# An adaLN block with a spectral filter and a gated feed-forward: the filtered product's planes added on GpSimd, mirrored W columns in rising order, powers on GpSimd, new orders

## The chip, the cores and the metric

The kernel runs on one core of one Trainium2 chip. The metric is the device time of one execution in microseconds. Engines are called PE (TensorE), PEld (its weight load), DVE (VectorE), ACT (ScalarE), POOL (GpSimd) and SP (SyncE, here the DMA queue).

## The reference, cut to what matters

```python
mod = (silu(c) @ w_mod).reshape(1, 6, 1, -1)      # sa, ca, ga, sb, cb, gb
h = layernorm(x) * (1 + ca) + sa                  # x: 1 x 2048 x 640
x = x + ga * irfft2(rfft2(h) * (w_r + 1j * w_i))  # filter over both axes
h = layernorm(x) * (1 + cb) + sb
x = x + gb * ((silu(h @ w_gate) * (h @ w_up)) @ w_down)   # 640 -> 1728 -> 640
```

All tensors are bfloat16; the transforms are done as matrix products with tables of cosines and sines.

## The kernel before, in words

The 2048 rows are 16 tiles of 128. Four stages follow each other, and each of the first three is driven by an order written out by hand: a string of short names, each of which issues the instructions of one step. An engine runs its own instructions in that order, so the string sets what stands behind what on every engine and on SP's DMA queue.

Stage 1 (to about 34 us) normalises the tiles and does the transform along the 640 axis and the first part of that along the rows; ACT writes the result into `A_sb`. GpSimd scales the table rows there (`gscale`, L305 and L306); tile 14's scaling runs on DVE.

Stage 2, the filter stage (34 to about 70 us), runs over 17 units (unit 16 is a small rest). For a unit `u`:
- `B`/`T`,`t`: turn a piece of `A_sb`, by a DMA transpose of two units (`B`, L424) or on PE with a copy (`T`, L431, and `t`, L437).
- `X`, `Xe`: eight matmuls with the tables (L451 to L459), copied from PSUM by ACT (L466).
- `P`: the product with the filter W on DVE, two instructions (L484): 768 elements a partition with columns of `Wb`, 512 with mirrored columns of `Wq`, which are read in falling order. The result `PP` has two planes that have to be summed.
- `Y`, `y`: five blocks turned by PE with the identity, two matmuls for each block, one for each plane, which sum in PSUM as float32 (L498, L502); the copy `y` goes to ACT for odd units and to DVE for even ones (L509).
- `E`, `e`: six matmuls with the inverse tables (L525 to L533) and a strided copy into `Ep` (L543), on ACT but for unit 14 and half of 15.

`J` and `Je` build `Wq` from `Wb` (matmuls L586, copies L589), `W` and `Jn` negate parts of the filter, `m` mirrors `Ep` (all L259 on DVE). `Ri` (L580) folds the gate ga into `Rinv_sb`; ga is turned and goes through DRAM to be spread over the partitions (L241, L247). `sb` and `cb` at the end compute two more modulation vectors on PE (L226). PSUM tiles come from a ring of four slots, so a step that needs a slot waits until the fourth one before it has been copied out.

Stage 3, the way back: `s` (ten matmuls, L659), `V` (ACT copy, L666), `d` (five matmuls, L672), `x` (DVE: add the input, with row sums, L675), `n` (mean, L679), `q` (ACT: squares, L683). `rt` takes the root for tiles 0 to 3 (ACT, then DVE's reciprocal and bias, L686 to L688), `xn`/`xa` normalise, `T`/`f` turn and scale them (L724, L728, L730). `gA` and `g0` to `g7` begin the feed-forward part of the first four tiles; `N` and a later call take the inverse roots of the other tiles on DVE by Newton steps (`ln2_newton`); `mb`, `mt` and `w` fold the gate gb into the down weights.

Stage 4 is the feed-forward part for the rest: `ffn_mm` (L764), `ffn_silu` (L769), `ffn_mul` (L773) and the down product (L852, L865), four passes of four tiles.

Of the kernel before, what the change touches and what calls it, by code (L numbers as in the profile page):

```python
# [22 lines left out]
NC5 = 5  # L23
# [82 lines left out]
def adaln_block_kernel(  # L106
# [29 lines left out]
    modcols = const.tile([P, 2, NC5], F32, name="modcols")  # L136
# [4 lines left out]
    neg1 = const.tile([P, 1], F32, name="neg1")  # L141
    ssq, vm = (const.tile([P, NT, 2], F32, name=n) for n in ("ssq", "vm"))
# [39 lines left out]
    nc.vector.memset(Wq[:, 3 * NT * 128:], 0.0)  # L182
    nc.vector.memset(Wqp[:, 1, 0:2048:64], 0.0)
# [36 lines left out]
    nc.gpsimd.memset(PP64[:], 0.0)  # L220
    nc.scalar.activation(warm[:], eps_t[:], ACT.Silu)
# [192 lines left out]
    with tc.tile_pool(name="ph2", bufs=2, reuse_waits="tile") as ph2, \  # L414
         tc.tile_pool(name="ps2", bufs=4, space=bass.MemoryType.PSUM, reuse_waits="tile") as ps2:
        B2all = big.tile([P, 8, NR, 128], BF16, name="B2all", tag="gt")
        B64 = ph2.tile([P, 2, 128], BF16, name="B64", bufs=1)
        X64 = ph2.tile([P, NI], BF16, name="X64", bufs=1)
# [14 lines left out]
        def copy_t(u):  # L433
            n = 640 if u < 16 else 256
            ps = pss.pop(("t", u))
            o = (B2all[:, u % 8] if u < 16 else B64[:]).rearrange("p b q -> p (b q)")
            (nc.vector.tensor_copy if u in (0, 1) else nc.scalar.copy)(o, ps[:, 0:n])  # L437
# [22 lines left out]
        def copy_x(u):  # L460
            xps = pss.pop(("x", u))
            if u == 16:
                nc.scalar.copy(X64[:], xps[:, 0, 0:NI])
                return
            X = Xs[u] = ph2.tile([P, NI, 4], BF16, name="X", bufs=6)
            nc.scalar.copy(X[:].rearrange("p q (b j) -> p q b j", b=2),  # L466
                           xps[:, :, 0:2 * NI].rearrange("p b (j q) -> p q b j", j=2))

        def product(u):
# [35 lines left out]
        def copy_y(u):  # L505
            yf = pss.pop(("y", u))[:].rearrange("p b q -> p (b q)")
# [28 lines left out]
        def copy_e(u):  # L535
# [5 lines left out]
            def put(s0, j0, n, copy=nc.vector.tensor_copy if u == 14 else nc.scalar.copy):  # L541
# [24 lines left out]
        def mods_cb(_):  # L566
            m = mods(wm_g, 1)
            nc.scalar.copy(modcols[:, 1, :], m)
            nc.scalar.add(one_p_cb[:], m, 1.0)

        def mods_sb(_):
            nc.scalar.copy(modcols[:, 0, :], mods(wm_sb, 0))
# [9 lines left out]
        def turn_w(h):  # L582
            ps = pss["j", h] = slot("wps")
            wv = Wb[:, 1 - h // 2, :, 0:256].rearrange("p k (m l) -> p k m l", m=2)
            for b in range(2):
                nc.tensor.matmul(ps[:, b, :], lhsT=jrev[:], rhs=wv[:, 8 * (h % 2) + 4 * b:8 * (h % 2) + 4 * b + 4, :, 64:128], start=True, stop=True)  # L586
# [5 lines left out]
        def loads(i):  # L592
# [49 lines left out]
    ps3 = ctx.enter_context(tc.tile_pool(name="ps3", bufs=4, space=bass.MemoryType.PSUM, reuse_waits="tile"))  # L642
    xsum, mean2, sq2, rstd2 = (const.tile([P, NT], F32, name=n) for n in ("xsum", "mean2", "sq2", "rstd2"))
# [3 lines left out]
    def ring(name):  # L647
        return ps3.tile([P, 2, 512], F32, name=name, tag="f")
# [29 lines left out]
    def ln2_mean(t):  # L678
        nc.vector.tensor_scalar(mean2[:, t:t + 1], xsum[:, t:t + 1], 1.0 / D, None, ALU.mult)  # L679

    def ln2_square(t):
        junk = ph4.tile([P, D], BF16, name="junk2", bufs=1)
        nc.scalar.activation(junk[:], x1[:, t, :], ACT.Square, scale=-1.0, bias=mean2[:, t:t + 1], accum_out=sq2[:, t:t + 1])  # L683

    def ln2_root(_):
        nc.scalar.activation(rstd2[:, 0:4], sq2[:, 0:4], ACT.Sqrt, bias=eps_t[:], scale=1.0 / D)  # L686
# [4 lines left out]
    def silu_table(_):
        nc.scalar.activation(warm[:], rstd2[:, 3:4], ACT.Silu)

    def ln2_newton(a, b):
        I32 = mybir.dt.int32
        n = b - a
        v = ph4.tile([P, 8], F32, name="veps")[:, 0:n]
        nc.vector.tensor_scalar(v, sq2[:, a:b], 1.0 / D, EPS, ALU.mult, ALU.add)
        yi = ph4.tile([P, 8], I32, name="rs_yi")[:, 0:n]
        nc.vector.tensor_single_scalar(yi, v.bitcast(I32), 1, ALU.arith_shift_right)  # L700
        nc.vector.tensor_scalar(yi, yi, -1, 0x5F3759DF, ALU.mult, ALU.add)
        y = yi.bitcast(F32)
        tt = ph4.tile([P, 8], F32, name="rs_t")[:, 0:n]
        for it in range(3):
            nc.vector.tensor_tensor(tt, y, y, ALU.mult)
            nc.vector.scalar_tensor_tensor(tt, tt, -0.5, v, ALU.mult, ALU.mult)
            nc.vector.scalar_tensor_tensor(rstd2[:, a:b] if it == 2 else y, tt, 1.5, y, ALU.add, ALU.mult)

    def ln2_xn(t):
# [3 lines left out]
        nc.vector.tensor_scalar(xn2s[sc][:, tl, :], x1[:, t, :], mean2[:, t:t + 1], rstd2[:, t:t + 1], ALU.subtract, ALU.mult)  # L713
# [66 lines left out]
    def gb_mods(_):  # L780
        mg_ps = ring("mg_ps")
        mod_cols(mg_ps[:, 0], wm_gb)
        nc.scalar.copy(g_col[1][:], mg_ps[:, 0, 0:MW * NC5:MW])
# [8 lines left out]
    def at_of(sc):  # L792
        if len(AT2) <= sc % 2:
# [6 lines left out]
             "m": lambda f: ffn_mul(AT2[0], f), "mA": lambda _: ffn_mul13(0, AT2[0]), "wm": silu_table, "N": lambda _: ln2_newton(4, 8), "mb": gb_mods, "mt": gb_turn, "w": fold}  # L800
    plan = (
# [152 lines left out]
```

## Time and profile before

| | us |
|---|---|
| median of 3 runs (lowest, highest) | 271.76 (271.46, 274.04) |
| the profiled execution | 272.35 |
| its span | 270.5 |
| PE, DVE, ACT, POOL busy | 260.0, 150.5, 122.2, 21.4 |
| granted clock | 1.00 |

The span is what the profile covers; the execution is 1.85 us longer. Times in the views count from the start of the span. A matmul's row shows its latency, while the next one starts before it has ended; what a step costs PE is therefore read from start to start. A group's row gives busy time, mean of one, then the idle time of the engine before it and what ended that.

### The profile page before, as it was taken

What the parts mean: (1) busy time and instruction counts of PE and PEld (TensorE: products, weight loads), DVE (VectorE), ACT (ScalarE), POOL (GpSimd) and SP (SyncE); (2) the same over time, 40 slices, a digit from 0 to 9 for tenths busy, and PEclk for the clock granted to TensorE, in tenths of its full rate; (3) what the DMA queues carried; (4) which work ended last, traced back from release to release, by engine and by line L of the source; (5) the groups of instructions that cost most, each with busy time, mean ns of one, the idle gap of its engine ahead of it and who ended that gap; (6) DMA issues with size and microseconds to landing.
All of it is one profiled execution on the core that took longest, in us unless ns stands there. A gap on an engine that the chain in (4) does not pass through costs nothing.

```text
span 270.5 us, 5340 instructions
## 1 busy us (share of the span) xinstructions
PE 260.0 (96%) x2190; PEld 168.3 (62%) x2190; DVE 150.5 (56%) x359; ACT 122.2 (45%) x221; POOL 21.4 (8%) x44
## 2 busy tenths in 40 slices
PE   6899999999978999999999999999999999999994
PEld 6788869988966555456644446654445664444663
DVE  2599979989388569984425452524344342333151
ACT  5499679898699976422033223022223103322000
POOL 3378800000000000000000000000000000000000
PEclk9999999999999999999999999999999999999999
DMA  7999457899397001040210004110004011000011
GB/s 245 334 344 357 138 142 175 220 233 335 104 396 283 10 14 24 0 97 2 74 34 13 0 0 97 51 58 10 2 0 97 2 73 34 12 0 0 0 51 48
DMA packets 35422, 27.80 MB, mean 103 GB/s; under 512 B 18117, under 2 KB 32710, under 8 KB 35270
## 3 DMA queue, kind: packets, MB, share of 16 engines
q1 hardware_dynamic: 35396, 27.46, 33.0%
q8 instruction: 17, 0.28, 0.4%
q14 instruction: 7, 0.06, 0.1%
q10 hardware_dynamic: 2, 0.00, 0.0%
HBM read 20.37 MB, written 2.62 MB: 85 GB/s over the span
## 4 chain that ended last, share of the span: by engine, by line
PE 75%; DMA 13%; DVE 4%; ACT 4%; SPq 2%; issue 1%; DVEq 0%; ACTq 0%
PE gu L764 42%; PE oa L865 20%; DMA Wb<-in_A_w_i_dram 5%; DMA x_sb<-in_A_x_dram 4%; PE va L659 2%; DMA wm_g<-in_w_mod_dram 2%; PE gu L751 2%; DMA ga_row<-gTa 1%; DVE late L675 1%; DMA ga_bc<-ga_row 1%; PE m_ps L226 1%; PE yps L498 1%; PE oa L852 1%; PE oab L672 1%; SPq L207 1%
## 5 line engine op out<-in xcount | busy, mean ns | idle before, releaser
L773 DVE TENSOR_TENSOR AT<-gu,sg 128x512 bf16<-128x512 f32 x52 | 35.8, 689 | 54.2 <-ACT sg L769 54.2
L764 PE MATMUL gu<-h2T_all,Wg 128*128 128x512 bf16 x260 | 64.6, 379 | 0.0
L764 PE MATMUL gu<-h2T_all,Wu 128*128 128x512 bf16 x260 | 64.6, 379 | 0.0
L769 ACT ACTIVATE sg<-gu 128x512 f32<-128x512 f32 x52 | 31.0, 596 | 70.0 <-PE gu L764 68.4
L865 PE MATMUL oa<-late,AT 128*128 128x320 bf16 x403 | 56.1, 299 | 0.0
L865 PEld LDWEIGHTS <-AT 128*128 128x128 bf16 x429 | 40.8, 98 | 17.2 <-issue 1.4
L764 PEld LDWEIGHTS <-Wu 128*128 128x128 bf16 x260 | 25.4, 98 | 30.7
L764 PEld LDWEIGHTS <-Wg 128*128 128x128 bf16 x260 | 25.1, 98 | 29.3
L879 DVE TENSOR_TENSOR xo<-oa,late 128x320 bf16<-128x320 f32 x31 | 20.0, 695 | 31.8 <-PE oa L852 18.6
L675 DVE SCALAR_TENSOR_TENSOR late<-oab,x_sb 128x640 bf16<-128x640 f32 x16 | 14.1, 884 | 10.2 <-PE oab L672 10.1
L753 ACT ACTIVATE sg<-gu 64x512 f32<-64x512 f32 x4 | 2.3, 586 | 37.2 <-PE gu L751 37.2
L305 POOL TENSOR_SCALAR Gs<-Gtab,rstd 128x256 bf16<-128x256 bf16 x15 | 13.8, 923 | 11.6 <-DVE rstd L300 8.2
L317 DVE SCALAR_TENSOR_TENSOR Z<-rtile,vm,z 128x640 bf16<-128x640 f32 x16 | 13.9, 872 | 0.4 <-PE z L312 0.3
L683 ACT ACTIVATE junk<-late,mean 128x640 bf16<-128x640 bf16 x16 | 13.2, 828 | 0.3
L330 ACT CAST A_sb<-aps 128x650 bf16<-128x650 f32 x16 | 11.1, 706 | 2.5 <-PE aps L326 2.3
L281 ACT COPY early<-t1ps 128x640 bf16<-128x640 bf16 x13 | 9.0, 692 | 5.9 <-PE t1ps L278 5.5
L466 ACT CAST X<-xps 128x640 bf16<-128x640 f32 x16 | 10.8, 696 | 1.6 <-PE xps L459 1.0
L659 PE MATMUL va<-Htab,Ep 128*128 128x128 bf16 x160 | 10.7, 219 | 0.8 <-ACT VT L666 0.4
L666 ACT CAST VT<-va 128x640 bf16<-128x640 f32 x16 | 10.5, 696 | 1.3 <-PE va L659 1.3
L659 PEld LDWEIGHTS <-Ep 128*128 128x128 bf16 x160 | 9.8, 118 | 1.0 <-issue 0.8
L498 PE MATMUL yps<-identb,PP 128*128 128x128 bf16 x130 | 9.7, 219 | 0.2 <-DVE Y L509 0.2
L325 PE MATMUL aps<-Z,Gs 128*128 128x325 bf16 x32 | 9.2, 303 | 0.0
(292 smaller groups left out, 337.6 us busy)
## 6 DMA issues: line engine op xcount, KB each, us to landing
x_sb<-in_A_x_dram SPq DMA_DIRECT2D x8, 320.0 KB, 6.2
out_dram<-xo SPq DMA_DIRECT2D x15, 160.0 KB, 1.7
Wu<-in_B_w_up_dram SPq DMA_DIRECT2D x1, 2080.0 KB
late<-in_B_w_down_dram SPq DMA_DIRECT2D x1, 2080.0 KB
wm_g<-in_w_mod_dram SPq DMA_DIRECT2D x2, 800.0 KB, 5.6
Wb<-in_A_w_r_dram SPq DMA_DIRECT2D x1, 1284.0 KB, 10.3
Wb<-in_A_w_i_dram SPq DMA_DIRECT2D x1, 1284.0 KB
Wg<-in_B_w_gate_dram SPq DMA_DIRECT2D x1, 1280.0 KB
```

The source lines that it names most:

```text
L305: e.tensor_scalar(Gss[t][:, 0:2], Gtab[:, t], rstd1[:, t:t + 1], None, ALU.mult)
L317: nc.vector.scalar_tensor_tensor(Zs[t][:].rearrange("p r q -> p (r q)"), rv, vm[:, t, 1:2], held.pop(("z", t))[:, 0:D], ALU.mult, ALU.add)
L330: (nc.vector.tensor_copy if t in A_DVE else nc.scalar.copy)(A_sb[:, :, t, :, :], i)
L498: nc.tensor.matmul(yf[:, 128 * j:128 * j + 128], lhsT=PP[:, cp, 0:128] if u == 16 else PP[:, cp, 0:128, j], rhs=identb[:], start=(cp == 0) ...
L659: nc.tensor.matmul(vf[:, 128 * r:128 * r + 128], lhsT=Ep[:, t, 65 - 65 * g:193 - 65 * g, r], rhs=Htab[:, t, g, :], start=(f == 1 and r in ...
L675: nc.vector.scalar_tensor_tensor(x1[:, t, :].rearrange("p (r a) -> p r a", r=NR), VTs.pop(t).rearrange("p (r a) -> p r a", r=NR), 1.0, x_s ...
L683: nc.scalar.activation(junk[:], x1[:, t, :], ACT.Square, scale=-1.0, bias=mean2[:, t:t + 1], accum_out=sq2[:, t:t + 1])
L764: nc.tensor.matmul(o, lhsT=w_[:, c5, fc * 128:(fc + 1) * 128], rhs=h2T_all[:, sc % 2, :, c5, :], start=(c5 == 0), stop=(c5 == NC5 - 1))
L769: nc.scalar.activation(gus[fc][1][:], gus[fc][0][:, 0, :], ACT.Silu)
L773: nc.vector.tensor_tensor(AT[:, fc, :], gu[:, 1, :], sg[:], ALU.mult)
L865: nc.tensor.matmul(o, lhsT=AT[:, fc, tl * 128:(tl + 1) * 128], rhs=Wd_sb[:, fc, h * 320 + d0:h * 320 + d0 + n], start=(fc == 0 and not ear ...
L879: nc.vector.tensor_tensor(xos[tl][:, h * 320:(h + 1) * 320].rearrange("p (a r) -> p a r", r=NR), ps[0][0].rearrange("p (a r) -> p a r", r= ...
```

## The change

- After the product, the two planes of `PP` are added: on GpSimd for eleven units (`Q_POOL`), on DVE for two (`Q_DVE`). For these thirteen, `Y` is five transposes of bf16 data into PSUM as bf16, instead of ten matmuls. `PP` has five buffers instead of four.
- `Wq` is built with the columns already reversed (the matmul `J` reads them with step -1), so that both products read rising columns.
- The copies are dealt out anew: `y` (`Y_ACT`), `t`, `e` (`E_DVE`) and `Je`. Units 2 and 3 are turned by a DMA transpose.
- The Silu table is loaded in stage 2 (`wm`); `sb` and `cb` stand at the head of stage 3's order; the loads of `wm_gb`, Wg and Wd are issued behind them, `wm_gb` first. The PSUM ring is kept over both stages. The write of the ga row goes out on ACT's queue, its spreading is a step of its own (`gs`).
- The inverse root for the second normalisation is an add and a power on GpSimd (`ln2_power`), with the 1/640 put into the squares; root, reciprocal and Newton steps go.
- Both orders are new.

The diff, cut:

```diff
-            for n, off, rows, wd, l, step in ((48, 0, Wbr, 128, l0, 1), (32, 48, Wqr, 64, 0, -1)):
+            for n, off, rows, wd in ((48, 0, Wbr, 128), (32, 48, Wqr, 64)):
...
+        def add(u):
+            PP = PPs[u]
+            (nc.gpsimd if u in Q_POOL else nc.vector).tensor_tensor(PP[:, 0], PP[:, 0], PP[:, 1], ALU.add)
+
         def stage_y(u):
             yps = pss["y", u] = slot("yps")
+            PP = PPs.pop(u)
+            if u in Q_POOL + Q_DVE:
+                yb = yps[:, 0, 0:320].bitcast(BF16)
+                for j in range(4):
+                    nc.tensor.transpose(yb[:, 128 * j:128 * j + 128], PP[:, 0, 0:128, j], identb[:])
+                nc.tensor.transpose(yb[:, 512:640], PP[:, 0, 128:NI].rearrange("p q j -> p (q j)"), identb[:])
+                return
...
         def turn_w(h):
             ps = pss["j", h] = slot("wps")
-            wv = Wb[:, 1 - h // 2, :, 0:256].rearrange("p k (m l) -> p k m l", m=2)
+            w = Wb[:, 1 - h // 2, 8 * (h % 2), 128]
             for b in range(2):
-                nc.tensor.matmul(ps[:, b, :], lhsT=jrev[:], rhs=wv[:, 8 * (h % 2) + 4 * b:8 * (h % 2) + 4 * b + 4, :, 64:128], start=True, stop=True)
+                nc.tensor.matmul(ps[:, b, :], lhsT=jrev[:], 
+                                 rhs=bass.AP(w.tensor, w.offset + 1536 * b, [w.ap[0], [384, 4], [128, 2], [-1, 64]]),
+                                 start=True, stop=True)
...
-        Y_ACT = (1, 3, 5, 7, 9, 11, 13, 15)
-        J_DVE = (0, 1)
+        Y_ACT = (0, 1, 3, 4, 8, 12, 13)
+        T_DVE, E_DVE = (1,), (3, 6, 14)
+        Q_POOL, Q_DVE = (3, 4, 5, 6, 7, 8, 9, 10, 11, 12, 14), (2, 15)
+        J_DVE = (0, 2)
...
+            "J2 T0 T1 t0 J3 Je3 Je2 t1 J0 W0 B2 B4 J1 X0 Je1 Je0 X1 Xe0 Jn W1 Xe1 P0 P1 ga X2 Xe2 gt X3 X4 X5 P2 Xe3 P3 B6 Y0 "
+            "Xe4 Xe5 Y1 Q2 y0 P4 Q3 y1 P5 X6 Xe6 E0 Y2 y2 Y3 Q4 e0 B8 B10 y3 X7 E1 X8 Xe7 W2 P6 e1 X9 Q5 Y4 Xe8 Xe9 Y5 W3 E2 "
+            "y4 e2 X10 P7 E3 P8 Xe10 Q6 y5 P9 e3 X11 T16 E4 Xe11 B12 P10 B14 Q7 Y6 t16 e4 y6 E5 P11 Y7 Q8 X12 Y8 e5 y7 E6 "
+            "Xe12 Q9 X13 y8 m0 e6 Q10 X16 X14 P12 Q11 L2 Y9 Xe13 Q12 y9 P13 Xe16 E7 L1 Xe14 e7 E8 e8 Y10 E9 X15 P16 Y11 y10 "
+            "P14 e9 Y12 Y13 y11 gs Xe15 P15 y12 E10 Y16 Ri E11 y13 Q14 E12 e10 Y14 Q15 e11 y16 L3 e12 Y15 E13 m1 wm y14 e13 "
+            "L4 E16 E14 y15 m2 e16 e14 m3 E15 e15 m4 "
...
+    def ln2_power(a, b):
+        nc.gpsimd.tensor_scalar(sq2[:, a:b], sq2[:, a:b], EPS, None, ALU.add)
+        nc.gpsimd.tensor_tensor(rstd2[:, a:b], sq2[:, a:b], mhalf[:, 0:b - a], ALU.pow)
...
+        "sb sx cb cx s0 s1 s2 V0 d0 s3 V1 s4 x0 V2 V3 n0 d1 d2 V4 q0 s5 x1 s6 n1 x2 V5 d3 n2 x3 V6 q1 d4 s7 d5 V7 s8 x4 "
+        "n3 q2 x5 d6 x6 V8 d7 q3 s9 d8 x7 s10 s11 V9 rt x8 nb V10 V11 s12 xn0 s13 n4 d9 xn1 x9 T0 V12 xn2 s14 V13 n5 xa3 "
+        "f0 T1 s15 V14 f1 d10 V15 mb mx gA d11 x10 x11 n6 n7 q4 g0 z0 mt g1 q5 z1 n8 g2 z2 m0 q6 m1 w0 d12 x12 mA n9 n10 "
+        "m2 q7 g3 g4 d13 n11 z3 m3 x13 q8 q9 w1 z4 m4 n12 g5 n13 w2 q10 N d14 q11 x14 z5 g6 m5 w3 q12 n14 d15 q13 x15 g7 "
+        "z6 n15 q14 q15 z7 m6 m7 "
```

More of the change, by code (lines that the diff above doesn't have):

```diff
@@ L412, in adaln_block_kernel @@
     NPE = 2
[L414 to L415 removed]
+    ps2 = ctx.enter_context(tc.tile_pool(name="ps2", bufs=4, space=bass.MemoryType.PSUM, reuse_waits="tile"))
+    with tc.tile_pool(name="ph2", bufs=2, reuse_waits="tile") as ph2:
         B2all = big.tile([P, 8, NR, 128], BF16, name="B2all", tag="gt")
[L417 to L418 removed]
+        B64 = rtile[:, 0:256].rearrange("p (b q) -> p b q", b=2)
+        X64 = rtile[:, 256:256 + NI]
         def slot(name):
@@ L462, in copy_x @@
             if u == 16:
-                nc.scalar.copy(X64[:], xps[:, 0, 0:NI])
+                nc.scalar.copy(X64, xps[:, 0, 0:NI])
                 return
@@ L564, in mods_ga, with silu_table @@
             nc.scalar.copy(g_col[0][:], mods(wm_g, 0))
[L566 to L572, printed above, removed]
         def ga_turn(_):
             gate_turn(slot("gT_ps")[0:NC5, 0, 0:64].bitcast(BF16), 0)
-            gate_spread(0)
+        def silu_table(_):
+            nc.scalar.activation(warm[:], eps_t[:], ACT.Silu)
         def rinv_gate(_):
@@ L678, in ln2_mean, with ln2_bias @@
     def ln2_mean(t):
-        nc.vector.tensor_scalar(mean2[:, t:t + 1], xsum[:, t:t + 1], 1.0 / D, None, ALU.mult)
+        nc.vector.tensor_scalar(mean2[:, t], over_d[:], xsum[:, t:t + 1], None, ALU.mult)
     def ln2_square(t):
         junk = ph4.tile([P, D], BF16, name="junk2", bufs=1)
-        nc.scalar.activation(junk[:], x1[:, t, :], ACT.Square, scale=-1.0, bias=mean2[:, t:t + 1], accum_out=sq2[:, t:t + 1])
+        nc.scalar.activation(junk[:], x1[:, t, :], ACT.Square, scale=-1.0 / D ** 0.5, bias=mean2[:, t, 1:2], accum_out=sq2[:, t:t + 1])
+    def ln2_power(a, b):
+        nc.gpsimd.tensor_scalar(sq2[:, a:b], sq2[:, a:b], EPS, None, ALU.add)
+        nc.gpsimd.tensor_tensor(rstd2[:, a:b], sq2[:, a:b], mhalf[:, 0:b - a], ALU.pow)
     def ln2_root(_):
-        nc.scalar.activation(rstd2[:, 0:4], sq2[:, 0:4], ACT.Sqrt, bias=eps_t[:], scale=1.0 / D)
-        nc.vector.reciprocal(rstd2[:, 0:4], rstd2[:, 0:4])
-        nc.vector.scalar_tensor_tensor(nb2[:], mean2[:, 0:4], -1.0, rstd2[:, 0:4], ALU.mult, ALU.mult)
+        ln2_power(0, 4)
         xn2s[0] = big.tile([P, 4, D], BF16, name="xn2c", tag="rs")
[L691 to L707, printed above, removed]
+    def ln2_bias(_):
+        nc.vector.scalar_tensor_tensor(nb2[:], mean2[:, 0:4, 0], -1.0, rstd2[:, 0:4], ALU.mult, ALU.mult)
     def ln2_xn(t):
@@ L778, in ffn_mul13, with late_mods, sb_out, cb_out @@
         nc.sync.dma_start(AT[64:128, 13, :], AT[0:64, 13, :])
[L780 to L783, printed above, removed]
+    mod_ps = {}
+    def late_mods(name, w, k=0, strided=True):
+        mod_ps[name] = ring("mg_ps")[:, 0]
+        mod_cols(mod_ps[name], w, k, strided)
+    def sb_out(_):
+        nc.scalar.copy(modcols[:, 0, :], mod_ps["sb"][:, 0:MW * NC5:MW])
+    def cb_out(_):
+        nc.scalar.add(one_p_cb[:], mod_ps["cb"][:, 0:MW * NC5:MW], 1.0)
+    def gb_out(_):
+        nc.scalar.copy(g_col[1][:], mod_ps["mb"][:, 0:MW * NC5:MW])
     def gb_turn(_):
@@ L810, in adaln_block_kernel @@
         steps[n](int(w[len(n):] or 0))
+        if w == "sb":
+            wm_gb = big.tile([P, NC5, D], BF16, name="wm_gb", tag="wsb")
+            nc.sync.dma_start(wm_gb[:], wm_v[:, :, 5 * D:6 * D])
+        if w == "cb":
+            Wg = big.tile([P, NC5, FFM], BF16, name="Wg", tag="wg")
+            for f0, f1 in ((0, 640), (640, FFM)):
+                nc.sync.dma_start(Wg[:, :, f0:f1], B_w_gate[:, f0:f1].rearrange("(dp c5) f -> dp c5 f", dp=P))
+            nc.sync.dma_start(Wd_sb[:, 0:13, :], B_w_down[0:FFM, :].rearrange("(fc fp) d -> fp fc d", fp=P))
+            for o in (0, 64):
+                nc.sync.dma_start(Wd_sb[o:o + 64, 13, :], B_w_down[FFM:FF, :])
     done = 8
```

63 lines of the change are left out of this document (28 added, 35 removed), and 11 rows, old and new, of the table plan.

## The prediction

> **What bounds the kernel now.** First I read the busy shares, then the windows of ten or twenty microseconds, then each engine's timeline in the stretch that the diff touches.
>
> ```profile
> PE 260.0 (96%) x2190; PEld 168.3 (62%) x2190; DVE 150.5 (56%) x359; ACT 122.2 (45%) x221; POOL 21.4 (8%) x44
> ```
>
> TensorE is the engine to relieve, and the shares of the others are averages over unlike stages. By window (busy us of PE, PEld, DVE, ACT, POOL):
>
> ```profile
> 40.00:60.00 20.00, 19.90 (x278) 17.93 (x276) 18.49 (x37) 18.33 (x33) 0.00 (x0) 1.00 0.81 203
> 60.00:70.00 10.00, 9.83 (x155) 9.02 (x153) 8.88 (x19) 7.83 (x15) 0.00 (x0) 1.00 0.71 247
> 70.00:80.00 10.00, 8.83 (x156) 8.58 (x155) 5.90 (x19) 8.44 (x17) 0.00 (x0) 1.00 0.84 291
> 80.00:90.00 10.00, 8.25 (x93) 5.89 (x92) 6.41 (x20) 9.67 (x19) 0.00 (x0) 1.00 0.64 238
> ```
>
> From 40 to 70 us (the filter stage: X, product, Y, E) PE is busy 29.7 of 30 us, but DVE (27.4) and ACT (26.2) stand close behind, and GpSimd does nothing. So time taken from PE alone is capped: after some 2.5 us DVE sets the end. From 70 to 90 us (the way back) PE idles 2.9 us. Behind that the feed-forward part runs gapless on PE and the diff leaves its work as it is. The granted clock is 1.00 throughout. Gains can come only from these two places and the seam before 40 us.
>
> **The change part by part, the filter stage.** The timeline of PE prices the pieces (start, duration):
>
> ```profile
> 38.15 0.30 PE L451 MATMUL xps<-Ktab,B2all 128*128 128x320 bf16 x1 [0.24 <-ACT Wq L589]
> ...
> 39.76 0.44 PE L431 MATMUL t2ps<-identb,A_sb 128*128 128x128 bf16 x5
> 40.04 0.30 PE L451 MATMUL xps<-Ktab,B2all 128*128 128x320 bf16 x1
> ...
> 43.80 0.61 PE L498 MATMUL yps<-identb,PP 128*128 128x128 bf16 x8
> 44.36 0.30 PE L451 MATMUL xps<-Ktab,B2all 128*128 128x320 bf16 x1
> ...
> 68.33 0.23 PE L533 MATMUL eps__1479<-KIt,Y 128*128 128x160 bf16 x1
> ```
>
> A Y step takes 44.36 - 43.80 = 0.56 us for ten matmuls (two of them on L502). With the planes added first it is five turns, and five turns take 40.04 - 39.76 = 0.28. Thirteen units change (2 to 12, 14, 15): 13 x 0.28 = 3.64 us off PE; T3 goes to a DMA transpose, 0.28 more (T2 too, ahead of the stretch). PE in 40 to 70 falls from 29.7 to 25.8.
>
> The prices of the other engines, from the groups by form (last figures: mean ns):
>
> ```profile
> L484 DVE TENSOR_TENSOR PP<-X,Wq 128x512 bf16<-128x512 bf16 x16 | 9.2, 576 | 0.0
> L484 DVE TENSOR_TENSOR PP<-X,Wb 128x768 bf16<-128x768 bf16 x16 | 8.8, 549 | 0.2 <-ACT X L466 0.2
> L509 DVE CAST Y<-yps 128x640 bf16<-128x640 f32 x8 | 6.5, 819 | 0.6 <-PE yps L502 0.5
> L437 DVE COPY B2all<-t2ps 128x640 bf16<-128x640 bf16 x2 | 0.9, 480 | 0.0
> L580 DVE TENSOR_TENSOR Rinv_sb<-Rinv_sb,ga_bc 128x640 bf16<-128x640 bf16 x1 | 0.5, 492 | 0.7 <-DMA ga_bc<-ga_row 0.7
> L509 ACT CAST Y<-yps 128x640 bf16<-128x640 f32 x8 | 5.6, 701 | 0.3 <-PE yps L502 0.2 <-ACT X L466 0.2
> L692 ACT ACT_TABLE_LOAD x1 | 1.3, 1283 | 0.0
> ```
>
> - Mirrored W columns: the 512-element product with falling columns (576 ns) costs more than the 768-element one with rising columns (549). The rising rows, 768 at 549 and 640 at 492, give about 435 for 512 (an estimate on their line). Saved: 16 x 0.14 = 2.3 us of DVE. Bounds 0 and 16 x 0.2.
> - Y copies: before, 8 on DVE at 0.82 (6.5). After, 9, all from bf16 PSUM, priced by the bf16 copy of the same size, 0.48: 4.3. Saved 2.2.
> - Added to DVE: the adds of units 2 and 15 (0.49 each by the Rinv row) and the E copies 3 and 6 (0.82 each by the f32 copy): 2.6. DVE nets -1.9: 25.5 instead of 27.4.
> - ACT loses those two E copies, one Y copy and t3 (four of about 0.70), and takes the Silu table load (1.28 + 0.2) out of the way back: 26.2 - 2.8 + 1.5 = 24.9.
> - The reversed reads move into the J matmuls (8 of them), which cost nothing more, or at most their own time again, 1.7 us; I take nothing, as PE has gaps around them.
>
> So three engines need 25 to 26 us where 30 were used. At PE's former fill that is 26 us; at DVE's former 91% it is 28.4. Without disturbance I take 27.3: a gain of 2.7.
>
> **GpSimd, the unknown.** No row shows a two-input add there. The nearest:
>
> ```profile
> L305 POOL TENSOR_SCALAR Gs<-Gtab,rstd 128x256 bf16<-128x256 bf16 x15 | 13.8, 923 | 11.6 <-DVE rstd L300 8.2 <-DMA Gtab<-tab_G 2.0 <-PE gps L285 0.7
> L306 POOL TENSOR_SCALAR Gs<-Gtab,rstd 128x128 bf16<-128x128 bf16 x15 | 5.6, 372 | 0.0
> L211 POOL TENSOR_SCALAR_AFFINE_SELECT identb<-identb 128x128 bf16<-128x128 bf16 x1 | 0.3, 292 | 0.1
> ```
>
> Taking 0.1 us as fixed, they run at 3.2, 2.1 and 1.5 ns an element: an add of 640 between 1.06 and 2.2 us; I take the middle row, 1.45. Eleven adds are 16 us, and Q3 to Q14 have some 18 us (44 to 62) to fit in, so they fit, barely; each lies between a product and a Y step that other units cover.
>
> What it does to DVE is seen in one place, where a GpSimd instruction and DVE's S14 run together:
>
> ```profile
> 32.29 0.29 DVE L305 TENSOR_SCALAR Gs<-Gtab,rstd 128x256 bf16<-128x256 bf16 x1
> 32.45 0.92 POOL L305 TENSOR_SCALAR Gs<-Gtab,rstd 128x256 bf16<-128x256 bf16 x1 [0.61 <-DVE rstd L300]
> 32.49 0.47 DVE L306 TENSOR_SCALAR Gs<-Gtab,rstd 128x128 bf16<-128x128 bf16 x1
> 32.89 0.87 DVE L317 SCALAR_TENSOR_TENSOR Z<-rtile,vm,z 128x640 bf16<-128x640 f32 x1
> ```
>
> Half the elements took 0.47 instead of 0.29 or less: about 0.2 us lost, though the DVE instruction still ended before GpSimd's. The next one, with an input in PSUM, takes its usual 0.87. Bounds: nothing, or 0.2 on each of the some 26 SBUF-only DVE instructions that meet an add, 5.2 us. I take one loss for each add, 11 x 0.2 = 2.2, so DVE rises to 27.7 and sets the stage at about 28.6. The filter stage then gains 1.4 us instead of 2.7.
>
> [...]
>
> **The seam before it.** X0 waits for a PSUM slot behind W copies:
>
> ```profile
> 34.55 0.59 PE L586 MATMUL wps<-Wb,jrev 128*128 128x512 bf16 x2
> ...
> 35.18 1.22 DVE L589 CAST Wq<-wps 128x1024 bf16<-128x1024 f32 x1 [0.68 <-PE wps L586]
> ...
> 37.09 1.01 ACT L589 CAST Wq<-wps 128x1024 bf16<-128x1024 f32 x1 [1.73 <-PE wps L586]
> ```
>
> Now its slot is that of T1, freed by t1 on DVE right after the first W copy: 35.18 + 1.22 + 0.48 = 36.9. PE has J3, J0, J1 to do until some 37.3. X0 moves from 38.15 to 37.3: 0.8 us (bounds 0 and 1.1). B2 is now the first DMA transpose, issued at the same moment as B4 before; seven issues instead of six precede the wm_sb and wm_g loads, which are wanted only at the end of the stage.
>
> **The way back.** PE's timeline and the chain to the first turn:
>
> ```profile
> 70.88 2.95 PE L659 MATMUL va<-Htab,Ep 128*128 128x128 bf16 x50 [0.33 <-ACT one_p_cb L569]
> ...
> 77.10 0.44 PE L672 MATMUL oab<-Rinv_sb,VT 128*128 128x128 bf16 x5 [0.47 <-DVE late L675]
> 77.91 0.72 PE L659 MATMUL va<-Htab,Ep 128*128 128x128 bf16 x10 [0.37 <-ACT VT L666]
> ...
> 81.82 0.81 PE L724 MATMUL h2ps<-identb,xn2c 128*128 128x128 bf16 x10 [1.45 <-DVE xn2c L713]
> ...
> 85.04 0.72 PE L659 MATMUL va<-Htab,Ep 128*128 128x128 bf16 x10
> 85.59 1.24 PE L751 MATMUL gu<-h2T_all,Wp 128*128 128x512 bf16 x5
> ...
> 95.10 0.94 PE L226 MATMUL mg_ps<-sc_col,wm_gb 128*128 128x64 bf16 x25
> ```
> ```profile
> 80.70 0.30 ACT L686 ACTIVATE rstd<-sq,eps_t 128x4 f32<-128x4 f32 x1
> 81.32 1.15 DVE L713 TENSOR_SCALAR xn2c<-late,mean,rstd 128x640 bf16<-128x640 bf16 x3
> ```
>
> An s step takes 0.55 us (85.04 to 85.59), a d step half of it. gA starts 14.7 us after s0 because T0 waits for the root and the normalised rows, and PE has nothing left to do. The new order puts s14, s15, d8, d9, d10 and mb ahead of gA: 1.1 + 0.84 + 0.8 = 2.7 us of work that came behind it. If gA starts as late as before, that is the gain; T0 may come later, since more VT copies stand ahead on ACT, by up to 1 us. The add and power on GpSimd take the place of ACT's root (0.30) and DVE's reciprocal: taken as equal, 0.5 us from the last square to xn0. No row shows a power; four columns are little if it runs like the rows above, and its price is open upward. I take 2.1 (bounds 0.5 and 2.9). Moving the powers for tiles 4 to 15 takes DVE work that PE does not wait for: nothing. The w0 fold stands ahead of x12 on DVE and waits for gb_bc; behind it x12 and m2 would be late, and then the slot of d13. g1 and g2, 4.3 us, cover most of it.
>
> **Sum.** Against the profiled execution's 272.35 us (span 270.5 and 1.85 around it): 1.4 + 0.8 + 2.1 = 4.3, so 268.05. The median of the runs shown lies 0.6 below that execution, so I give 267.5 for a median.
>
> **The rivals.**
> - DVE pays for GpSimd in full: 25.5 + 5.2 = 30.7 us busy, at 96% fill 32. The filter stage loses 2.0, the seam and the way back give 2.9: 270.9. For it: the 0.47 row; against it: that this is one row, of another form. "Same".
> - GpSimd becomes the bound. Adds at 2.2 us (the L305 rate) with 0.4 of waiting behind DVE's two-input products are 2.6 each: from 44 us on, Q14 ends at 72.6, and Y14, E14, e14 and the mirror behind it need some 3 us, so the stage ends at 75.6 instead of 70.2. Less 2.1 of the way back, the total is 275. It makes the kernel slower once an add takes over 2.3 us in all (44 + 11 x 2.3 + 3 = 72.3). For it: GpSimd's slowest row lies just under that, and PE's Y steps follow in a fixed order, so a late add holds all behind it. Against it: the other two rows.
> - The relief does not arrive: PE waits for ACT and DVE copies in the fixed order, and the stage keeps its 30 us. Only seam and way back count: 269 or a little over, on the edge of faster.
> - Power is dear: each microsecond over 0.5 at the root delays T0 and gA by as much; at 4 us the gain is gone, 271.5. [...]
>
> **How the numbers follow.** A measurement of this kernel can tell about 1% from no change (268.9 and 274.4). Forecast 0.48, nearly all of it faster; relief not arriving 0.18, two thirds faster; DVE paying in full 0.14, same; power 0.04, same; GpSimd the bound 0.16, slower. Faster 0.61, same 0.22, slower 0.17. Everything at its good bound (4 + 1.1 + 2.9) gives 264.3, less 0.6 for the median; the upper end takes in the full payment and part of the slow GpSimd: 263.5 to 273. The forecast's own range is 264 to 269.
>
> **What would show it.** Right: yps groups of 5 at 0.28 us; products on Wq near 0.44 (when no add runs); Y copies on DVE at 0.48; adds of about 1.45 on POOL; the last E matmul near 66 instead of 68.4; gA about 14.7 to 15.3 after s0 with d11 next behind it. Wrong: PE waiting for POOL PP in the list of waits; Wb products well over 0.55; E15 at 68 or later; a gap of over 2 us before T0.

## The result, and the profile after

The changed kernel takes 275.46 us (median of 4 runs, 275.22 to 276.46) where the kernel before took 272.16 (271.46 to 274.04) beside it: ratio 1.0141, 95% interval 1.0095 to 1.0187 (the quotient of the two medians, 1.0121, lies inside it). It is slower by 1.4%, and the forecast of 267.5 us, with a range to 273, was wrong. The profiled execution took 275.22 us, with a span of 273.2 and a mean granted clock of 0.992.

The busy shares of the changed kernel, then its windows (span of the window, then busy us of PE, PEld, DVE, ACT, POOL; granted clock; DMA share; GB/s):

```profile
PE 256.9 (94%) x2115; PEld 164.3 (60%) x2115; DVE 156.2 (57%) x336; ACT 120.1 (44%) x215; POOL 42.0 (15%) x64
```
```profile
40.00:60.00 20.00, 14.81 (x170) 12.60 (x169) 19.72 (x27) 13.21 (x22) 11.79 (x8) 0.91 1.03 264
60.00:70.00 10.00, 7.89 (x100) 6.79 (x99) 10.00 (x18) 6.91 (x12) 4.19 (x3) 1.00 0.37 123
70.00:80.00 10.00, 9.08 (x164) 8.93 (x165) 7.25 (x18) 7.89 (x16) 0.00 (x0) 1.00 0.47 143
80.00:90.00 10.00, 8.79 (x143) 8.10 (x141) 8.76 (x26) 10.00 (x20) 1.27 (x2) 1.00 1.05 368
```

PE was relieved as planned: 22.7 us busy from 40 to 70 where it had 29.7. But the stage did not become shorter, because DVE is now busy for 29.7 of these 30 us. DVE runs fewer instructions in them than before (45 instead of 56, from the counts in brackets), so each must have become longer. The groups by form show which:

```profile
L486 DVE TENSOR_TENSOR PP<-X,Wb 128x768 bf16<-128x768 bf16 x16 | 16.4, 1025 | 0.5 <-ACT X L469 0.5
L495 POOL TENSOR_TENSOR PP<-PP 128x640 bf16<-128x640 bf16 x11 | 16.0, 1452 | 21.0 <-DVE PP L486 20.1 <-PE eps__1086 L546 0.9
L486 DVE TENSOR_TENSOR PP<-X,Wq 128x512 bf16<-128x512 bf16 x16 | 9.0, 566 | 0.0
```

The unchanged product on Wb has a mean of 1025 ns instead of 549. GpSimd's add itself is as cheap as forecast, and GpSimd idles for 20 us until products of DVE end (half of that ahead of the first add); it is not the bound. The timelines of GpSimd and of DVE, side by side (start, duration), show how one add meets one product:

```profile
41.87 1.58 POOL L495 TENSOR_TENSOR PP<-PP 128x640 bf16<-128x640 bf16 x1 [9.73 <-DVE PP L486]
44.34 1.58 POOL L495 TENSOR_TENSOR PP<-PP 128x640 bf16<-128x640 bf16 x1 [0.90 <-DVE PP L486]
46.34 1.39 POOL L495 TENSOR_TENSOR PP<-PP 128x640 bf16<-128x640 bf16 x1 [0.42 <-DVE PP L486]
```
```profile
42.10 1.76 DVE L486 TENSOR_TENSOR PP<-X,Wb 128x768 bf16<-128x768 bf16 x1
43.79 0.41 DVE L486 TENSOR_TENSOR PP<-X,Wq 128x512 bf16<-128x512 bf16 x1
44.12 0.54 DVE L486 TENSOR_TENSOR PP<-X,Wb 128x768 bf16<-128x768 bf16 x1
44.59 1.61 DVE L486 TENSOR_TENSOR PP<-X,Wq 128x512 bf16<-128x512 bf16 x1
46.12 0.48 DVE L522 COPY Y<-yps 128x640 bf16<-128x640 bf16 x1
46.53 1.52 DVE L262 TENSOR_SCALAR Wb<-Wb,neg 128x768 bf16<-128x768 bf16 x1
```

The add ends at 43.45; the product that began at 42.10 ends at 43.86, 0.41 us after it, where such a product by itself takes 0.55. The next two products take their usual 0.41 and 0.54 (the second was already running when the next add began), and the copy from PSUM its 0.48, although an add begins beside it. So each add holds one DVE instruction until the add is done. In the whole stage eleven DVE instructions are held in this way, one for each add: seven products on Wb, two on Wq and two negations, at 1.32 to 1.76 us each; every one ends 0.28 to 0.42 us after its add. Taken over the stage: 16 x (1025 - 550) = 7.6 us on Wb, 16 x (566 - 419) = 2.4 on Wq (550 and 419 are the same groups of the version with all adds on DVE, below), and 1.0 on each of the two negations: 12.0 us, 1.1 for each add.

PE, which takes its steps in a fixed order, waits for what is late behind the held products. The list of waits of PE between 36 and 75 us:

```profile
PE xps L454 <- DVE Y L522: 2.5, 2, 1.3
PE eps__1036 L541 <- DVE Y L522: 2.0, 1, 2.0
PE yps L503 <- DVE Ep L556: 1.8, 2, 1.2
PE yps L503 <- DVE Y L522: 1.8, 2, 1.1
```

The way back begins at 74.89 us instead of 70.88, 4.0 later. It gives 1.1 us back, and the feed-forward part behind it takes 0.2 less, which leaves the span's 2.7. The start of the way back understates the loss, because the filter stage also began earlier. Its first matmul X0 and the first matmul s0 of the way back in the changed kernel:

```profile
35.91 0.30 PE L454 MATMUL xps<-Ktab,B2all 128*128 128x320 bf16 x1
74.89 1.85 PE L659 MATMUL va<-Htab,Ep 128*128 128x128 bf16 x30
```

From X0 to s0 the stage takes 74.89 - 35.91 = 38.98 us, where the kernel before took 70.88 - 38.15 = 32.73: it is 6.25 us longer.

### The profile page after: what moved, and what is told of

It is laid out like the page before. It is cut to its first block, busy times and chain, and to the rows that moved or that the text cites. A ratio compares the mean times of both kernels' runs of the same rounds, so it can differ in the third digit from the quotient of the medians.

```text
span 273.2 us, 5196 instructions
## 1 busy us (share of the span) xinstructions
PE 256.9 (94%) x2115; PEld 164.3 (60%) x2115; DVE 156.2 (57%) x336; ACT 120.1 (44%) x215; POOL 42.0 (15%) x64
## 4 chain that ended last, share of the span: by engine, by line
PE 71%; DMA 11%; DVE 10%; ACT 3%; issue 2%; SPq 2%; ACTq 0%; DVEq 0%
PE gu L751 41%; PE oa L873 20%; DVE PP L486 5%; DMA Wb<-in_A_w_i_dram 5%; DMA x_sb<-in_A_x_dram 4%; DMA wm_g<-in_w_mod_dram 2%; PE gu L738 2%; ACT VT L666 1%; DVE Y L522 1%; PE mg_ps L229 1%; PE va L659 1%; PE oa L860 1%; DVE late L675 1%; SPq L207 1%; PE oab L672 1%
## 5 line engine op out<-in xcount | busy, mean ns | idle before, releaser
L495 POOL TENSOR_TENSOR PP<-PP 128x640 bf16<-128x640 bf16 x11 | 16.0, 1452 | 21.0 <-DVE PP L486 20.1
L486 DVE TENSOR_TENSOR PP<-X,Wb 128x768 bf16<-128x768 bf16 x16 | 16.4, 1025 | 0.5 <-ACT X L469 0.5
## 6 DMA issues: line engine op xcount, KB each, us to landing
late<-in_B_w_down_dram SPq DMA_DIRECT2D x1, 2080.0 KB, 16.6
```

What stands on the lines that cost most here:

```text
L486: nc.vector.tensor_tensor(bass.AP(o.tensor, o.offset, [o.ap[0], [4 * NI, 2], [2 * NI, 2], [4, n], [1, 4]]), bass.AP(xi.tensor, xi.offset, ...
L495: (nc.gpsimd if u in Q_POOL else nc.vector).tensor_tensor(PP[:, 0], PP[:, 0], PP[:, 1], ALU.add)
```

## The experiments

Two theories were tested. *Held*: a two-input GpSimd add holds a DVE instruction that reads SBUF until the add ends, and that alone made the kernel slower. *Order*: the new order, or the chain product, add, turn, is what delays PE.

**Adds on DVE, on PE, or left out.** Three versions of the changed kernel with its order kept.

```diff
-        Q_POOL, Q_DVE = (3, 4, 5, 6, 7, 8, 9, 10, 11, 12, 14), (2, 15)
+        Q_POOL, Q_DVE = (), (2, 3, 4, 5, 6, 7, 8, 9, 10, 11, 12, 14, 15)   # adds on DVE
+        Q_POOL, Q_DVE = (), ()                                            # ten matmuls for each unit
...
+            if u in Q_POOL:                                               # adds left out: in add(u), Q_POOL as in the changed kernel
+                return
```


> The changed kernel with all thirteen adds on DVE, order unchanged. Theory 'held' (a GpSimd add holds every DVE instruction whose inputs all lie in SBUF until it ends, 11 times about 1.1 us): the long products (1.3 to 1.76 us) and negations (1.5) go back to 0.55 and 0.52, DVE gains 11 x 0.4 us of adds, the filter stage is about 8 us shorter less what PE and ACT then need: 268 to 270.5 us. Rival 'order' (the new order makes DVE, ACT and PE wait for PSUM slots whatever GpSimd does): within 1.5 us of the changed kernel, 274 to 277, with the same gaps on PE.

> The changed kernel with no adds: PE sums the planes of all units as before (ten matmuls), order, rising columns and way back unchanged. Theory 'held': PE needs 3.6 us more, DVE's copies are float32 again (0.82 for 0.48), nothing is held: 268.5 to 271 us. Rival 'order': 274 or more, since PE has more work in the same bad order.

> The changed kernel with the eleven GpSimd adds left out: for those units only the first plane is turned, so the second plane's part is missing from the result. It shows what the change would give if GpSimd's adds cost nothing. Theory 'held': the filter stage runs at 27 to 28 us instead of 37, total 265 to 268. Rival 'order': 273 or more.

Measured: adds on DVE 268.32 us (ratio 0.9893, 0.9877 to 0.9909), planes on PE 268.6 (0.99, 0.9885 to 0.9916), adds left out 265.82 (0.9804, 0.9781 to 0.9828). The windows from 40 to 60 us and 60 to 70 us, in this order of the versions:

```profile
40.00:60.00 20.00, 18.28 (x235) 15.71 (x233) 19.54 (x49) 16.60 (x30) 0.00 (x0) 1.00 1.03 281
60.00:70.00 10.00, 9.68 (x156) 8.62 (x154) 7.36 (x18) 8.06 (x17) 0.00 (x0) 1.00 0.49 138
```
```profile
40.00:60.00 20.00, 20.00 (x283) 18.23 (x281) 18.15 (x38) 17.02 (x31) 0.00 (x0) 1.00 1.05 268
60.00:70.00 10.00, 9.88 (x167) 9.19 (x165) 7.15 (x15) 7.69 (x15) 0.00 (x0) 1.00 0.51 155
```
```profile
40.00:60.00 20.00, 20.00 (x268) 17.89 (x266) 18.89 (x46) 18.77 (x34) 0.00 (x0) 1.00 1.05 279
60.00:70.00 10.00, 9.21 (x164) 8.80 (x163) 6.26 (x15) 8.00 (x16) 0.00 (x0) 1.00 0.73 215
```

All three beat both kernels with the new order in place, so the new order by itself does not make the kernel slower. With adds on DVE, DVE does 49 instructions in the 20 us in which it did 27, and its products are back at their old length:

```profile
L486 DVE TENSOR_TENSOR PP<-X,Wb 128x768 bf16<-128x768 bf16 x16 | 8.8, 550 | 0.5 <-ACT X L469 0.5
L486 DVE TENSOR_TENSOR PP<-X,Wq 128x512 bf16<-128x512 bf16 x16 | 6.7, 419 | 0.0
```

From X0 to s0 the three versions take 31.55, 31.88 and 29.20 us. The last, with the adds left out:

```profile
36.38 0.30 PE L454 MATMUL xps<-Ktab,B2all 128*128 128x320 bf16 x1
65.58 1.85 PE L661 MATMUL va<-Htab,Ep 128*128 128x128 bf16 x30
```

The difference of the spans with and without the GpSimd adds, 273.2 - 263.9, says what eleven adds cost at the end: 9.3 us (9.1 by the ratios, 1.0141 - 0.9804 of 271.1).

**The pair by itself.** Four equal DVE instructions of 640 elements start about 0.05 us after one GpSimd instruction of 640 (two-input add, multiply of one input by a constant, copy, memset) or after none.

```python
for d in (d_pair, d_one, d_wide, d_step, d_ps, d_mix):   # DVE: two bf16 inputs; one; two f32; one f32 with step 2; PSUM; PSUM and SBUF
    for p in (None, p_add, p_mul1, p_copy, p_set):       # GpSimd
```


> Not the block: a copy of x to the output and thirty small cells. In each, four equal DVE instructions of 640 elements start some 0.2 us after one GpSimd instruction of 640 elements. DVE forms: pair (two bf16 inputs in SBUF), one (one bf16 input in SBUF), wide (two float32 inputs), step (one float32 input with step 2), ps (copy from PSUM), mix (one input in PSUM, one in SBUF). GpSimd: none, add (two inputs), mul (one input), copy, memset. Theory 'held': the first of the four takes until the add's end, about 1.2 us more, in pair, one and wide; ps and mix are untouched; one-input GpSimd work holds less. Rival 'shared bandwidth': all of the instructions that run during the add get slower by a factor, none waits for its end. Rival 'order': no cell shows more than 0.2 us.

The timeline of DVE, the tile's name telling the pair (start, duration of all four), and GpSimd's groups:

```profile
11.71 1.70 DVE L64 TENSOR_TENSOR pair_none<-x 128x640 bf16<-128x640 bf16 x4 [0.35 <-ACT pair_none L46]
14.06 2.90 DVE L64 TENSOR_TENSOR pair_add<-x 128x640 bf16<-128x640 bf16 x4 [0.51 <-ACT pair_add L46]
17.60 2.23 DVE L64 TENSOR_TENSOR pair_mul<-x 128x640 bf16<-128x640 bf16 x4 [0.50 <-ACT pair_mul L46]
23.32 1.70 DVE L64 TENSOR_TENSOR pair_set<-x 128x640 bf16<-128x640 bf16 x4 [0.50 <-ACT pair_set L46]
25.57 1.27 DVE L67 TENSOR_SCALAR one_none<-x,one 128x640 bf16<-128x640 bf16 x4 [0.41 <-ACT one_none L46]
27.49 2.42 DVE L67 TENSOR_SCALAR one_add<-x,one 128x640 bf16<-128x640 bf16 x4 [0.50 <-ACT one_add L46]
30.55 2.24 DVE L67 TENSOR_SCALAR one_mul<-x,one 128x640 bf16<-128x640 bf16 x4 [0.50 <-ACT one_mul L46]
35.80 1.62 DVE L67 TENSOR_SCALAR one_set<-x,one 128x640 bf16<-128x640 bf16 x4 [0.50 <-ACT one_set L46]
74.49 3.02 DVE L76 CAST ps_none<-ps 128x640 bf16<-128x640 f32 x4 [0.41 <-ACT ps_none L46]
78.15 3.02 DVE L76 CAST ps_add<-ps 128x640 bf16<-128x640 f32 x4 [0.50 <-ACT ps_add L46]
```
```profile
L52 POOL TENSOR_SCALAR a<-a 128x640 bf16<-128x640 bf16 x6 | 11.2, 1859 | 14.2 <-ACT wide_mul L46 3.5 <-ACT step_mul L46 2.3 <-ACT ps_mul L46 2.3
L49 POOL TENSOR_TENSOR a<-a 128x640 bf16<-128x640 bf16 x6 | 8.3, 1390 | 40.8 <-ACT pair_add L46 13.6 <-ACT mix_add L46 6.6 <-ACT ps_add L46 5.9
```

Beside the add of 1.39 us, DVE loses 1.2 us, with two inputs or one. Beside the one-input multiply, which takes longer (1.81 us), products lose only 0.53, and beside a memset nothing (1.70 for the four with and without it). DVE's one-input form loses 0.97 to the multiply and 0.35 to the memset. The DVE copies that read PSUM lose nothing at all (3.02 with and without the add). The add loses nothing itself here: it takes 1.39 us beside each of the six DVE forms. The list of the pair of products and add says which of the four instructions pays (ns, shortest, median, longest):

```profile
L64 DVE TENSOR_TENSOR pair_add<-x x4: 479/480/1696, 14.1 to 16.5; 128x640 bf16<-128x640 bf16 x4
```

Only the first does: it ends at 15.76, 0.36 us after the add, and the other three take 0.48 as without it. This answers a third theory, that DVE and GpSimd share bandwidth and everything beside the add slows by some factor: the first instruction, which takes 0.48 us without the add, still took 0.36 from the add's end at 15.40.

**The adds alone.** The kernel before, its order and columns kept, with eleven adds on GpSimd.

```diff
+            if u in Q_POOL:   # at the end of product(u); Y and y as in the changed kernel
+                nc.gpsimd.tensor_tensor(PP[:, 0], PP[:, 0], PP[:, 1], ALU.add)
```


> The kernel before with one part of the change only: eleven planes added on GpSimd and turned as one, the old order and the falling columns kept. Theory (a GpSimd add with two inputs holds every SBUF-only DVE instruction beside it until it ends, about 1.1 us for each add): DVE, which has 27.4 of 30 us in the filter stage, loses 2.0 on six Y copies and gets 12 more, so the stage takes 37 to 38 us: 278 us, range 275 to 282, products on DVE with a mean near 0.9 us. Rival (the new order or the new columns made the kernel slower, the adds are cheap): PE is relieved of 3.1 us and DVE of 2.0, so 268 to 271.5 us, products as before.

Measured: 280.21 us, ratio 1.0334 (1.0297 to 1.0372). Its groups by form:

```profile
L484 DVE TENSOR_TENSOR PP<-X,Wb 128x768 bf16<-128x768 bf16 x16 | 14.2, 885 | 2.4 <-ACT X L466 2.4
L484 DVE TENSOR_TENSOR PP<-X,Wq 128x512 bf16<-128x512 bf16 x16 | 12.7, 796 | 0.0
```

Both products grow, by 16 x (336 + 220) ns = 8.9 us. It is slower than the changed kernel: it has nothing of the rest of the change, and PE waits here for the adds themselves as well, as its list of waits shows:

```profile
PE yps L500 <- POOL PP L491: 5.6, 4, 2.1
```

In the changed kernel's list no wait for GpSimd stands, so there the chain through the add is not what PE waited for. In this version it is part of the loss.

**Rising columns alone.** The kernel before with the mirrored W columns in rising order.

```diff
-            for n, off, rows, wd, l, step in ((48, 0, Wbr, 128, l0, 1), (32, 48, Wqr, 64, 0, -1)):
+            for n, off, rows, wd in ((48, 0, Wbr, 128), (32, 48, Wqr, 64)):   # J reads with step -1
```


> The kernel before with one part of the change only: mirrored W columns kept in rising order. Both theories expect products on Wq at 0.42 us instead of 0.58. Theory (PE, busy 29.7 of 30 us, sets the filter stage of the kernel before, so 2.3 us less on DVE are nearly worthless there): 271 us, 270.5 to 271.8. Rival (DVE sets the stage as much as PE): 269 to 270.2 us.

Measured: 270.72 us, ratio 0.9984 (0.9968 to 0.9999). The group:

```profile
L481 DVE TENSOR_TENSOR PP<-X,Wq 128x512 bf16<-128x512 bf16 x16 | 6.7, 422 | 0.0
```

DVE gets 2.5 us back and the kernel 0.4, and from X0 to s0 the stage takes 32.72 us, as before: PE set the stage. What this part saves is worth something only once PE is relieved.

**Five adds on GpSimd.** Units 4, 6, 8, 10 and 12 there, the other eight on DVE.

```diff
+        Q_POOL, Q_DVE = (4, 6, 8, 10, 12), (2, 3, 5, 7, 9, 11, 14, 15)
```


> The changed kernel with five of the eleven GpSimd adds (units 4, 6, 8, 10, 12), the other eight on DVE. Theory (each add on GpSimd costs DVE its own 1.1 us instead of the 0.48 of an add on DVE, whatever its neighbours): 268.3 (all adds on DVE) plus 5 x 0.65, so 271.5 us, range 270 to 273. Rival (GpSimd's queue of adds, one behind the other, is what delayed PE; with twice the room the adds cost nothing): 267.5 to 268.8 us.

Measured: 271.12 us, ratio 1.0001 (0.9989 to 1.0014). Five adds cost 2.9 us over adds on DVE (1.0001 - 0.9893 of 271.2), 0.59 each; eleven cost 6.7 (1.0141 - 0.9893), 0.61 each. The price goes with the number of adds, also where GpSimd has twice the room.

**Memsets and one-input multiplies in place of the adds.** The same places in the order, the same first planes, and Y still waits for GpSimd; the second planes of these eleven units are left out of the result.

```diff
-            (nc.gpsimd if u in Q_POOL else nc.vector).tensor_tensor(PP[:, 0], PP[:, 0], PP[:, 1], ALU.add)
+            for _ in range(2): nc.gpsimd.memset(PP[:, 0], 0.0)                 # first version, units of Q_POOL
+            nc.gpsimd.tensor_scalar(PP[:, 0], PP[:, 0], 2.0, None, ALU.mult)   # second version, units of Q_POOL
```


> The changed kernel with each of the eleven GpSimd adds replaced by two GpSimd memsets of the same plane (0.63 us each by the measurement of pairs, so 1.26 us where the add had 1.39); the second planes of those units are left out and the first are zero. GpSimd stays as busy and a Y step still waits for it. Theory (the add holds DVE because both fetch operands from SBUF; a memset fetches none): products at 0.55 and 0.42 us, time as without the adds, 266 us, range 265.5 to 267.5. Rival (GpSimd in the chain from product to turn, or any GpSimd instruction beside DVE, is what costs): 273 to 276 us.

> The changed kernel with each of the eleven GpSimd adds replaced by a multiply of the same plane by a constant: one input, 1.81 us by the measurement of pairs; the second planes of those units are left out and the first are scaled. Theory (the price hangs on the form of the GpSimd instruction; beside a two-input DVE product a one-input multiply costs 0.53 us, so 11 of them some 6 us of DVE and, at the 9.6 / 12 that reached the end with the adds, 4.7 us): 270.5 us, range 269 to 273. By the prediction's term of 0.2 us for each: 267.5. Rival (GpSimd's time as such, longer here than with adds): 277 us or more.

Measured: memsets 265.76 us (0.98, 0.9786 to 0.9815), multiplies 269.59 (0.9939, 0.9922 to 0.9955). The groups, first of the memsets, then of the multiplies:

```profile
L497 POOL MEMSET PP<- 128x640 bf16 x22 | 14.4, 674 | 12.6 <-DVE PP L486 9.8 <-PE yps L508 2.2
L486 DVE TENSOR_TENSOR PP<-X,Wb 128x768 bf16<-128x768 bf16 x16 | 8.8, 551 | 0.5 <-ACT X L469 0.5
```
```profile
L496 POOL TENSOR_SCALAR PP<-PP 128x640 bf16<-128x640 bf16 x11 | 21.0, 1928 | 10.5 <-DVE PP L486 10.5
L486 DVE TENSOR_TENSOR PP<-X,Wb 128x768 bf16<-128x768 bf16 x16 | 11.1, 693 | 0.4 <-ACT X L469 0.4
```

With 14.4 us of memsets in the chain the kernel is as fast as without adds; with 21.0 us of multiplies, more GpSimd time than the adds' 16.0, by the ratios (1.0141 and 0.9939) it is 5.5 us faster than with the adds. Neither GpSimd's time nor the chain through it is what cost. The price goes with the form of its instruction: by the ratios nothing for two memsets, (0.9939 - 0.9804) of 271.1 = 3.7 us for eleven multiplies of one input, 9.1 for eleven adds of two.

**The power left out.** The version with all adds on DVE, with a straight line in place of the inverse root.

```diff
-        nc.gpsimd.tensor_scalar(sq2[:, a:b], sq2[:, a:b], EPS, None, ALU.add)
-        nc.gpsimd.tensor_tensor(rstd2[:, a:b], sq2[:, a:b], mhalf[:, 0:b - a], ALU.pow)
+        nc.gpsimd.tensor_scalar(rstd2[:, a:b], sq2[:, a:b], -0.5, 1.5, ALU.mult, ALU.add)
```


> The version with all adds on DVE, with the powers left out: one GpSimd tensor_scalar (a straight line in place of the root) instead of the add and the power. Theory (PE takes T0 in its fixed order with no wait for the root, so the power's 1.04 us is off the path): the first gate matmul of g8 stays 36.4 us after s0, span 266.3 within 0.4. Rival (the root sets T0 and gA): T0 some 0.9 to 1.1 us earlier against s0 and the span 265.3.

In the one execution measured, the span is 266.4 against 266.3 with the power, and gA starts 16.4 us after s0 in both. The power takes 1.04 us and makes the chain from the last square to xn0 1.6 us long, where the kernel before has 1.1, but it is off the path.

**A balance.** Nine adds on DVE, units 5 to 8 with ten matmuls, the E copy of unit 6 on ACT, nothing on GpSimd.

```diff
+        T_DVE, E_DVE = (1,), (3, 14)
+        Q_POOL, Q_DVE = (), (2, 3, 4, 9, 10, 11, 12, 14, 15)
```


> The changed kernel with no add on GpSimd: nine planes added on DVE, units 5 to 8 summed by PE with ten matmuls, the E copy of unit 6 back on ACT. Theory (with DVE adds everywhere DVE is full from 50 to 60 us, with none PE is full to 66 us; a share for each evens them out): 267.2 us, range 266.3 to 268. Rival (the order written out sets the stage, not the load of one engine): 268.3 to 268.8 us as in the two pure versions.

> The balanced version again (nine adds on DVE, units 5 to 8 summed by PE, no add on GpSimd, E copy 6 on ACT), with more rounds, since its first interval was 1.2 per cent wide while its profiled span, 265.0, was 1.3 us under that of all adds on DVE. Theory (a share for each engine): 267.2 us, ratio 0.983 to 0.988. Rival (the gain of the profiled execution does not stand): 268.3 us, ratio 0.989 to 0.991.

Measured: 267.9 us (0.9898, 0.9839 to 0.9957), and measured a second time 267.1 (0.9854, 0.9839 to 0.9869). That is the fastest version with the whole computation, 4.0 us below the kernel before. Its window of the stage, with PE near full and DVE and ACT close behind:

```profile
40.00:70.00 30.00, 29.49 (x427) 26.60 (x425) 26.69 (x63) 26.20 (x48) 0.00 (x0) 1.00 0.94 249
```

## Why the prediction was wrong, point by point

**The step that failed** is the contention: "I take one loss for each add, 11 x 0.2 = 2.2", with an upper bound of 5.2. It measured 12.0 us of DVE, 1.1 for each add. The prediction let this term take 1.3 us from the filter stage (a gain of 1.4 instead of 2.7); it took 9.3 from the kernel. The 0.2 came from one row in which the GpSimd instruction had *one* input, and DVE's instruction ended before it, at 32.96 against 33.37; none of the eleven that an add held ended before the add. The multiplies show what that row was good for: beside them a product loses about half a microsecond (0.53 of 1.81 in the run of pairs), and the kernel comes to 269.59, still 2 us above the forecast, as eleven of them cost 3.7 us at the end. A two-input add is another form with another price (1.2 of 1.39 there). The sum was generous in one more step: it put DVE's 27.7 us at a stage of 28.6, a fill of 97%, where the former 91% would have given 30.4 and no gain; this step held, as DVE came out busy for 29.7 of 30 us. The rival "DVE pays for GpSimd in full" named the engine that pays, but priced it from the same row, as 0.2 on each of 26 instructions instead of 1.1 on one for each add. "GpSimd becomes the bound" gave 275, close to the time by luck: its mechanism did not occur. No run shows its 2.6 us for an add (2.2, and 0.4 of waiting behind DVE's products): with the waiting in it, the mean of an add was 1.45 us in the changed kernel, 1.48 in the kernel before with the adds alone and 1.65 with five adds. Nor did the relief fail to arrive: without adds on GpSimd the stage is shorter, at 29.20 to 31.88 us from X0 to s0 instead of 32.73.

**The gain without disturbance** was right as a sum, in part by luck. Its terms 2.7 + 0.8 + 2.1 = 5.6 us stand against 5.3 measured with the adds left out (1 - 0.9804 of 271.1). But the filter stage gained 32.73 - 29.20 = 3.5 us instead of 2.7 there, and the way back 1.1 instead of 2.1: the two misses nearly cancel. Of the prices, five turns instead of ten (0.28 us from start to start), rising columns at 0.42 us (0.435 forecast), bf16 copies at 0.48 and DVE adds at 0.48 (0.49) came as priced. So did the GpSimd add itself: 1.45 us taken, 1452 ns measured. That hit is luck in part, because the row it was scaled from has one input, and a one-input multiply of the same 640 elements takes 1928 ns.

**The seam:** from the start of the last stage-1 matmul to X0 took 3.92 us before and 3.34 after, 0.6 us against 0.8. The profiled X0 itself came 2.2 us earlier (35.91); the rest of that is a stage 1 that ended earlier. Its last matmul starts at 34.23 in the kernel before and at 32.57 in the changed kernel, but also at 33.34 in the kernel before with the adds alone and at 33.73 in the changed kernel with multiplies. One execution each does not tell how much of this, if any, the change brought.

**The way back** brought 1.1 of the 2.1 us: from s0 to the first matmul of g8 it is 37.44 us before and 36.37 after, the same in all versions with the new order. "If gA starts as late as before" was the wrong step. The windows from s0 to gA, before and after:

```profile
70.88:85.59 14.71, 12.12 (x200) 11.40 (x200) 9.65 (x30) 13.73 (x26) 0.00 (x0) 1.00 0.97 348
```
```profile
74.89:91.26 16.37, 15.10 (x265) 14.26 (x263) 12.69 (x36) 15.37 (x29) 1.27 (x2) 1.00 0.95 320
```

PE had 2.6 us of gaps before gA, not enough room for the 3.0 us of work that was moved ahead, and 1.3 of gaps remain: ACT is busy for 15.4 of the 16.4 us, and in the version with all adds on DVE three of PE's four waits in this stretch (0.2 to 0.3 us each) are for what ACT writes. The gain is about the gaps that were closed.

**The power** was taken as equal to the old root, with 0.5 us from the last square to xn0. That chain took 1.1 us before and takes 1.6 now, and the 0.5 more cost nothing. The fold w0 did wait for gb_bc, 1.3 us, and PE did not wait for it.

**Sum:** 5.3 gained, 9.3 lost, 4.0 slower; measured 1.0141 of 272, 3.8 us.

## What to carry to other kernels

An idle engine is not free help (here eleven adds on GpSimd cost 9.3 us): before work is moved to it, price its effect on the busy neighbour with the same form of instruction, number of inputs and source memory included, in a run of four instructions if the trace has no such row. A bound taken from another form of instruction is no bound: here it was 5.2 us of DVE, and 12.0 were measured. And where relieving one engine makes a second one the limit, the relief should be dealt out between them: here some sums on PE and some on DVE, with one E copy back on ACT, beat either alone (ratio 0.9854 against 0.99 and 0.9893).

## What the runs showed of the hardware that was not expected

A DVE instruction with one SBUF input pays for a GpSimd add as much as one with two does (1.27 to 2.42 us for four, 1.70 to 2.90), while one that reads PSUM is left alone even when its second input is in SBUF (3.02 us with and without the add).

The wait goes both ways. In the changed kernel the four adds that begin while DVE is inside an instruction on SBUF take 1.49 to 1.58 us; the seven that begin beside a copy from PSUM take 1.39 or 1.40.

With eleven adds on GpSimd PE's granted clock fell below 1.00 inside the stage, where PE had gaps: from 40 to 60 us it was 0.91 in the changed kernel, and in the kernel before with the adds alone it was 0.66 from 55 to 60 us. In the profiled executions with five adds and with multiplies, where PE had gaps too but fewer (16.6 and 18.1 us busy from 40 to 60, against 14.8), it stayed at 1.00. Why is open. Little of the time seems to hang on it: with five adds, at a clock of 1.00, an add cost 0.59 us over one on DVE, and with eleven 0.61.
